# A fused attention and gated feed-forward kernel: direct loads and turns, packed score slabs, new order of the stages

## The chip, the cores and the metric

One core of one Trainium2 chip. The metric is device time in microseconds (us); the kernel before takes 592.26 us (median of three runs, 591.85 to 592.28).

## The reference

Eight batches, eight heads, 576 queries of 64 numbers. Sixteen beacon keys and values stand ahead of the 576 own ones, and a query sees all beacons and the own keys up to its own place. The eight heads' outputs side by side make one token of 512 numbers; 4608 such tokens then go through a gated feed-forward layer of width 1536.

```python
scores = scale * np.matmul(q, k_all.transpose(0, 1, 3, 2))      # k_all = beacon_k, then k
scores = np.where(causal, -1000000000.0, scores)
a = np.exp(scores - scores.max(-1, keepdims=True))
a /= a.sum(-1, keepdims=True) + 1e-09
x = np.matmul(a, v_all).transpose(0, 2, 1, 3).reshape(B * S, H * D)
out = (np.maximum(x @ w_gate, 0.0) * (x @ w_val)) @ w_out
```

## The kernel before, in words

Work goes by pairs of heads: 8 batches of 4 pairs. The loads are all issued by GpSimd (L207, L225), which turns fp32 into bf16 on the way: 24 to 28 transfers a batch, in runs of one head row (64 numbers). Batch 0 is issued first, then the weights (wg and wv in quarters, wo whole), and a whole batch ahead of each batch's first step. The io tiles have two buffers, so batch b+1 is issued when batch b begins.

For each pair TensorE turns q and k (L236, L244; five transposes each) into qT and kT. Four steps follow, each with a score matmul for both heads (L254, `qk`; key rows by query columns, so the scores come out transposed), an exponential on ScalarE (L261), a mask by affine_select on GpSimd (L264), and one step later the product with v (L283, `av`). There the values are the weights of the matmul and the exponentials move through; a second matmul with 64 columns of ones makes the sums of the exponentials on 64 partitions. VectorE then takes the reciprocal of these sums (L290), multiplies (L292) into xT, which is already in the layout that the feed-forward layer wants, and SyncE writes one row of reciprocals to rsum (L294).

The feed-forward layer has nine tiles of 512 tokens (`ffn_tile`). A tile is twelve "ups" (four matmuls with wg at L308, Relu on ScalarE at L311, four matmuls with wv at L314, a product on VectorE at L316) and four "downs" (twelve matmuls at L323, a copy at L326, a store from SyncE at L327). From batch 1 on, one of the sixteen pieces of the preceding tile is put after each attention step: each engine runs its instructions in the order of this program, and a wait of one holds up what stands behind it. Two tiles are left for the end, and before the last but one a count is made of sums that are within range (`count_in_range`); if any is not, a slow general path runs after everything else.

Of the kernel before, what the change touches and what calls it, by code (L numbers as in the profile page):

```python
# [21 lines left out]

STEPS = (
# [5 lines left out]
)  # L29
STEP_COLS = (416, 512, 416, 320)  # L30

CHUNKS = ((0, 256, 0, 0), (256, 256, 1, 2), (512, 64, 3, 3))
CHUNK_OF_STEP = (0, 1, 1, 2)
# [109 lines left out]

@with_exitstack
def kernel(
# [23 lines left out]
    TAIL = Stot - 4 * P  # L169
    M_TILE = 512  # L170
    scale = 1.0 / (D ** 0.5)
    assert (Nb, S, D) == (16, 576, 64)
# [3 lines left out]
    make_identity(nc, ident)  # L176
    ones = const.tile([P, D], BF16, name="ones")
    nc.vector.memset(ones, 1.0)
# [4 lines left out]

    rsum = const.tile([2 * B * NP, S], FP32, name="rsum")

    main = ctx.enter_context(ExitStack())
    io = main.enter_context(tc.tile_pool(name="io", bufs=2))
    tsb = main.enter_context(tc.tile_pool(name="tsb", bufs=2))
    psb = main.enter_context(tc.tile_pool(name="psb", bufs=3))
    nrm = main.enter_context(tc.tile_pool(name="nrm", bufs=3))  # L190
# [3 lines left out]
    aux_ps = main.enter_context(tc.tile_pool(name="aux_ps", bufs=2, space=bass.MemoryType.PSUM))  # L194
    f_ps = main.enter_context(tc.tile_pool(name="f_ps", bufs=2, space=bass.MemoryType.PSUM))


    def load_qkv(b, h0, h1, tiles):
        q_sb, k_sb, v_sb = tiles
        c0, c1 = h0 * D, h1 * D  # L200

        def four(dst, t0, t1, src):
            for t in range(t0, t1):
                part(dst, 0, P, t, src[:, (t - t0) * P:(t - t0 + 1) * P])

        def part(dst, p0, p1, t, src):
            nc.gpsimd.dma_start(  # L207
                dst[p0:p1, t, c0:c1].rearrange("p (h d) -> p h d", d=D),
                src.rearrange("h p d -> p h d"))

        first = P - Nb
        for dst, src, beacon in ((k_sb, k, beacon_k), (v_sb, v, beacon_v)):
            part(dst, 0, Nb, 0, beacon[b, h0:h1])
            part(dst, Nb, P, 0, src[b, h0:h1, 0:first])
            four(dst, 1, 4, src[b, h0:h1, first:first + 3 * P])
            part(dst, 0, TAIL, 4, src[b, h0:h1, first + 3 * P:S])
            if dst is k_sb:
                four(q_sb, 0, 4, q[b, h0:h1, 0:4 * P])
                part(q_sb, 0, S - 4 * P, 4, q[b, h0:h1, 4 * P:S])

    def io_tiles():
        return tuple(io.tile([P, NKT, d_model], BF16, name=n) for n in ("q_sb", "k_sb", "v_sb"))

    def load_w(dst, src, n0, n1):
        nc.gpsimd.dma_start(dst[:, :, n0:n1],  # L225
                            src.rearrange("(ko ki) n -> ki ko n", ki=P)[:, :, n0:n1])


    class Pair:
        pass  # L230

    def prep_q(pr):
        tp = aux_ps.tile([P, 1024], BF16, name="aux")
        for t in range(NKT):
            n = P if t < 4 else S - 4 * P
            nc.tensor.transpose(tp[:, t * P:t * P + n], pr.q[:n, t, pr.c], ident[:n, :n])  # L236
        pr.qT = tsb.tile([P, S], BF16, name="qT")
        nc.vector.tensor_copy(pr.qT, tp[:, :S])

    def prep_k(pr):  # L240
        tp = aux_ps.tile([P, 1024], BF16, name="aux")
        for t in range(NKT):
            n = P if t < 4 else TAIL
            nc.tensor.transpose(tp[:, t * P:t * P + n], pr.k[:n, t, pr.c], ident[:n, :n])  # L244
        pr.kT = tsb.tile([P, NKT * P], BF16, name="kT")
        nc.vector.tensor_copy(pr.kT[:, :Stot], tp[:, :Stot])  # L246
        nc.gpsimd.memset(pr.kT[:, Stot:], 0.0)

    def qk(pr, i):
        s = s_ps.tile([P, 2, 512], FP32, name="s")  # L250
        for (kt, q0, n, c, _, _) in STEPS[i]:
            for a in range(2):
                rows = slice(a * D, (a + 1) * D)
                nc.tensor.matmul(s[:, a, c:c + n], pr.kT[rows, kt * P:(kt + 1) * P],  # L254
                                 pr.qT[rows, q0:q0 + n], start=True, stop=True)
        pr.s[i] = s

    def softmax(pr, i):
        n = STEP_COLS[i]
        p = psb.tile([P, 2, 512], BF16, name="p")  # L260
        nc.scalar.activation(p[:, :, :n], pr.s[i][:, :, :n], AF.Exp, scale=scale)  # L261
        for (kt, q0, _, c, m, base) in STEPS[i]:
            if m:
                nc.gpsimd.affine_select(  # L264
                    out=p[:, :, c:c + m], in_=p[:, :, c:c + m],
                    pattern=[[0, 2], [1, m]], compare_op=ALU.is_ge, fill=0.0,
                    base=base, channel_multiplier=-1)
        pr.p[i] = p

    def av(pr, i):  # L270
        ci = CHUNK_OF_STEP[i]
        cq0, cn, first, last = CHUNKS[ci]
        if i == first:
            pr.o[ci] = aux_ps.tile([P, 2, 256], FP32, name="aux")
        o = pr.o[ci]
        p = pr.p[i]
        for j, (kt, q0, n, c, _, _) in enumerate(STEPS[i]):
            kr = P if kt < 4 else TAIL
            for half in range(2):
                for a in range(2):  # L280
                    rows = slice(a * D, (a + 1) * D)
                    w = pr.v[:kr, kt, pr.c0 + a * D:pr.c0 + (a + 1) * D] if half == 0 else ones[:kr, :]
                    nc.tensor.matmul(  # L283
                        o[rows, half, q0 - cq0:q0 - cq0 + n], w, p[:kr, a, c:c + n],
                        start=(i == first and j == 0 and half == 0),
                        stop=(i == last and j == len(STEPS[i]) - 1),
                        skip_group_check=True)
        if i == last:
            r = nrm.tile([P, 256], FP32, name="r")
            nc.vector.reciprocal(r[:, :cn], o[:, 1, :cn])  # L290
            t0 = pr.b * S + cq0
            nc.vector.tensor_mul(xT[:, pr.p_idx, t0:t0 + cn], o[:, 0, :cn], r[:, :cn])  # L292
            g = 2 * (pr.b * NP + pr.p_idx)
            nc.sync.dma_start(rsum[g:g + 2, cq0:cq0 + cn],  # L294
                              r.rearrange("(a x) n -> a x n", a=2)[:, 0, :cn])


    def ffn_tile(m):
        m0 = m * M_TILE
        st = {}  # L300

        def up(nf):
            def go():
                if nf == 0:
                    st["h"] = fsb.tile([P, NF, M_TILE], BF16, name="hT")
                g = f_ps.tile([P, M_TILE], FP32, name="f")
                for ki in range(KM):
                    nc.tensor.matmul(g, wg[:, ki, nf * P:(nf + 1) * P], xT[:, ki, m0:m0 + M_TILE],  # L308
                                     start=(ki == 0), stop=(ki == KM - 1))
                gs = fsb.tile([P, M_TILE], FP32, name="g")  # L310
                nc.scalar.activation(gs, g, AF.Relu)  # L311
                u = f_ps.tile([P, M_TILE], FP32, name="f")
                for ki in range(KM):
                    nc.tensor.matmul(u, wv[:, ki, nf * P:(nf + 1) * P], xT[:, ki, m0:m0 + M_TILE],  # L314
                                     start=(ki == 0), stop=(ki == KM - 1))
                nc.vector.tensor_mul(st["h"][:, nf, :], gs, u)  # L316
            return go

        def down(ms):
            def go():  # L320
                o = f_ps.tile([P, d_model], FP32, name="f")
                for nf in range(NF):
                    nc.tensor.matmul(o, st["h"][:, nf, ms * P:(ms + 1) * P], wo[:, nf, :],  # L323
                                     start=(nf == 0), stop=(nf == NF - 1))
                ob = osb_p.tile([P, d_model], FP32, name="ob")
                nc.scalar.copy(ob, o)  # L326
                nc.sync.dma_start(out[m0 + ms * P:m0 + (ms + 1) * P, :], ob)  # L327
            return go

        return [up(nf) for nf in range(NF)] + [down(ms) for ms in range(M_TILE // P)]  # L330

    n_m = n_tokens // M_TILE

    def count_in_range():

# [14 lines left out]
    with tc.manual_schedule():  # L350
# [17 lines left out]
        def bind(pr):  # L368
            pr.q, pr.k, pr.v = tiles[pr.b]
# [69 lines left out]
```

## Time and profile before

| | |
|---|---|
| median of three runs | 592.26 us |
| span of the profiled execution | 589.1 us |
| around the span (median less span; no other time of that execution is listed) | 3.2 us |
| TensorE matmul busy | 447.3 us (76%) |
| VectorE / ScalarE / GpSimd busy | 259.4 / 194.9 / 218.1 us |
| mean granted TensorE clock | 0.945 |

The profile is one execution on the chip. Busy times of TensorE hold the latency of each matmul, so the time from one group's start to the next says more than the mean of one. The chain of waits goes back from the last instruction, at each step to what released it.

### The profile page before, as it was taken

The numbers are of one execution on the slowest core, as the hardware profiler recorded it, in microseconds if no ns is written. First come the engines' busy times: TensorE is split into PE (matmuls) and PEld (weight loads), VectorE is DVE, ScalarE is ACT, GpSimd is POOL, SyncE is SP. The second block draws the span as 40 slices with busy tenths as digits, with TensorE's granted clock in tenths as the row PEclk, the third lists the DMA queues.
The fourth block names the chain that finished last, engine by engine and source line by source line (L and its number), as shares of the span: only waits on it lengthen the run. The fifth ranks groups of instructions, "written<-read, shape, count | busy, mean of one in ns | idle before, by whom it ended". The sixth has DMA issues, their size and how long they took to land.

```text
span 589.1 us, 10169 instructions
## 1 busy us (share of the span) xinstructions
PE 447.3 (76%) x4113; PEld 227.8 (39%) x4113; DVE 259.4 (44%) x369; ACT 194.9 (33%) x273; POOL 218.1 (37%) x458
## 2 busy tenths in 40 slices
PE   2000037859995999599969986997799999979995
PEld 1000025525542554355435543553355555424442
DVE  0000027536733673376437543754476576432130
ACT  2000014324432543254425442543244454322321
POOL 9998262471246125621652174217411112000000
PEclk9999999779997999799979996999699999979998
DMA  4669990190059006900890099009901100100102
GB/s 31 40 41 138 202 115 2 14 112 2 3 94 102 1 3 102 94 1 20 96 82 2 21 108 69 2 22 120 57 2 38 39 1 10 65 0 19 53 2 75
DMA packets 127029, 29.45 MB, mean 50 GB/s; under 512 B 116608, under 2 KB 122368, under 8 KB 126976
## 3 DMA queue, kind: packets, MB, share of 16 engines
q0 software_dynamic: 121408, 19.15, 44.4%
q1 hardware_dynamic: 5568, 9.59, 4.4%
q8 instruction: 34, 0.56, 0.4%
q14 instruction: 19, 0.16, 0.1%
HBM read 38.27 MB, written 9.44 MB: 81 GB/s over the span
## 4 chain that ended last, share of the span: by engine, by line
PE 66%; POOL 23%; DMA 6%; DVE 2%; issue 1%; ACT 1%; ACTq 0%; POOLq 0%; DVEq 0%
PE f L308 16%; PE f L314 15%; PE f L323 14%; PE aux L283 11%; POOL v_sb L207 8%; POOL k_sb L207 7%; PE s L254 6%; POOL q_sb L207 5%; DMA wo<-in_moe_w_out_dram 4%; PE aux L236 2%; DMA k_sb<-in_k_dram 2%; PE aux L244 2%; DVE r L290 1%; POOL p L264 1%; ACT p L261 1%
## 5 line engine op out<-in xcount | busy, mean ns | idle before, releaser
L290 DVE RECIPROCAL r<-aux 128x256 f32<-128x256 f32 (+1 forms) x96 | 129.8, 1352 | 160.8 <-PE aux L283 160.7
L261 ACT ACTIVATE p<-s 128x832 bf16<-128x832 f32 (+2 forms) x128 | 110.4, 863 | 245.3 <-PE s L254 245.3
L264 POOL TENSOR_SCALAR_AFFINE_SELECT p<-p 128x224 bf16<-128x224 bf16 (+3 forms) x224 | 67.7, 334 | 273.2 <-ACT p L261 273.2
L283 PE MATMUL aux<-p,v_sb 128*64 128x64 bf16 (+5 forms) x832 | 72.9, 240 | 116.3 <-POOL p L264 111.0
L308 PE MATMUL f<-xT,wg 128*128 128x512 bf16 x432 | 119.5, 400 | 5.0 <-DVE xT L292 4.3
L316 DVE TENSOR_TENSOR hT<-g,f 128x512 bf16<-128x512 f32 x108 | 74.0, 685 | 107.5 <-PE f L314 105.6
L314 PE MATMUL f<-xT,wv 128*128 128x512 bf16 x432 | 114.5, 389 | 0.9 <-DVE hT L316 0.9
L283 PEld LDWEIGHTS <-v_sb 128*64 128x64 bf16 (+1 forms) x832 | 45.6, 116 | 167.6 <-issue 160.1
L323 PE MATMUL f<-wo,hT 128*128 128x512 bf16 x432 | 98.4, 380 | 0.0
L311 ACT ACTIVATE g<-f 128x512 f32<-128x512 f32 x108 | 64.4, 596 | 70.1 <-PE f L308 68.7
L314 PEld LDWEIGHTS <-wv 128*128 128x128 bf16 x432 | 43.4, 100 | 64.4 <-issue 19.3
L283 PE MATMUL aux<-p,ones 128*64 128x64 bf16 (+5 forms) x832 | 64.9, 234 | 0.0
L323 PEld LDWEIGHTS <-hT 128*128 128x128 bf16 x432 | 40.1, 98 | 46.7 <-issue 1.5
L308 PEld LDWEIGHTS <-wg 128*128 128x128 bf16 x432 | 36.9, 100 | 41.6 <-issue 10.6
L254 PE MATMUL s<-qT,kT 64*128 64x64 bf16 (+3 forms) x832 | 49.2, 233 | 0.6 <-DVE kT L246 0.6
L207 POOL DMA_DIRECT2D q_sb<-in_q_dram x55 | 44.2, 890 | 8.0 <-DMA wo<-in_moe_w_out_dram 6.8
L207 POOL DMA_DIRECT2D k_sb<-in_k_dram x55 | 43.8, 858 | 5.7 <-DMA wg<-in_moe_w_gate_dram 3.5
L283 PEld LDWEIGHTS <-ones 128*64 128x64 bf16 (+1 forms) x832 | 45.2, 118 | 0.2
L326 ACT COPY ob<-f 128x512 f32<-128x512 f32 x36 | 21.1, 585 | 72.3 <-PE f L323 72.3
L207 POOL DMA_DIRECT2D v_sb<-in_v_dram x55 | 44.3, 907 | 1.7 <-DMA k_sb<-in_k_dram 1.5
L292 DVE TENSOR_TENSOR xT<-aux,r 128x256 bf16<-128x256 f32 (+1 forms) x96 | 34.3, 358 | 3.3
L254 PEld LDWEIGHTS <-kT 64*128 64x128 bf16 x832 | 25.1, 99 | 12.0 <-issue 7.1
(26 smaller groups left out, 119.4 us busy)
## 6 DMA issues: line engine op xcount, KB each, us to landing
out_dram<-ob SPq DMA_DIRECT2D x36, 256.0 KB
q_sb<-in_q_dram POOLq DMA_DIRECT2D x28, 128.0 KB, 5.7
k_sb<-in_k_dram POOLq DMA_DIRECT2D x21, 128.0 KB, 5.1
v_sb<-in_v_dram POOLq DMA_DIRECT2D x21, 128.0 KB, 4.7
wg<-in_moe_w_gate_dram POOLq DMA_DIRECT2D x4, 384.0 KB, 8.9
wv<-in_moe_w_val_dram POOLq DMA_DIRECT2D x4, 384.0 KB, 10.1
wo<-in_moe_w_out_dram POOLq DMA_DIRECT2D x1, 1536.0 KB, 20.7
rsum<-r SPq DMA_DIRECT2D x64, 2.0 KB
```

The lines of the kernel that those rows point to most:

```text
L207: nc.gpsimd.dma_start(dst[p0:p1, t, c0:c1].rearrange("p (h d) -> p h d", d=D), src.rearrange("h p d -> p h d"))
L254: nc.tensor.matmul(s[:, a, c:c + n], pr.kT[rows, kt * P:(kt + 1) * P], pr.qT[rows, q0:q0 + n], start=True, stop=True)
L261: nc.scalar.activation(p[:, :, :n], pr.s[i][:, :, :n], AF.Exp, scale=scale)
L264: nc.gpsimd.affine_select(out=p[:, :, c:c + m], in_=p[:, :, c:c + m], pattern=[[0, 2], [1, m]], compare_op=ALU.is_ge, fill=0.0, base=base, ...
L283: nc.tensor.matmul(o[rows, half, q0 - cq0:q0 - cq0 + n], w, p[:kr, a, c:c + n], start=(i == first and j == 0 and half == 0), stop=(i == la ...
L290: nc.vector.reciprocal(r[:, :cn], o[:, 1, :cn])
L292: nc.vector.tensor_mul(xT[:, pr.p_idx, t0:t0 + cn], o[:, 0, :cn], r[:, :cn])
L308: nc.tensor.matmul(g, wg[:, ki, nf * P:(nf + 1) * P], xT[:, ki, m0:m0 + M_TILE], start=(ki == 0), stop=(ki == KM - 1))
L311: nc.scalar.activation(gs, g, AF.Relu)
L314: nc.tensor.matmul(u, wv[:, ki, nf * P:(nf + 1) * P], xT[:, ki, m0:m0 + M_TILE], start=(ki == 0), stop=(ki == KM - 1))
L316: nc.vector.tensor_mul(st["h"][:, nf, :], gs, u)
L323: nc.tensor.matmul(o, st["h"][:, nf, ms * P:(ms + 1) * P], wo[:, nf, :], start=(nf == 0), stop=(nf == NF - 1))
```

## The change

Nearly every stage is written anew; the feed-forward arithmetic and the general path stay.

Loads. For batches 0 and 1, k and q come with 9 (or 6 and 3) successive rows in one run, and are turned on TensorE in 64 by 64 pieces (`direct`, `pair_turn`). For batches 2 to 7 the fp32 rows come by SyncE's queue into a stage of six buffers, GpSimd casts them to bf16 (`cast`), and a transposing DMA from SyncE's queue turns them into kq (`turn`). v is staged and cast too. Weights still come by GpSimd's queue, in four parts of columns and wo in three.

Attention. A unit is one pair and one of two groups of queries, 0 to 367 or 368 to 575. Score columns stand in slabs; from batch 2 three slabs are made at once, and one slab may hold parts of two units. The mask is a product with a 0/1 tile on VectorE (`tri`). In `av` the exponentials are now the weights and v with a column of ones is what moves (65 columns), so the sums come out one per query, on its own partition; the reciprocal is of 4 to 6 numbers per partition. The result has tokens on partitions and is turned into xT, by a transposing DMA, or on TensorE for batch 0 and the first group of batch 2.

Order. Feed-forward tiles have 368 and 208 tokens, so that each is ready with its group of queries; downs go by 128 tokens as before. A planner puts ups and downs between attention steps, so that enough is left up to when the next tile is ready; exponentials, masks and `av` stand between pieces of it. PSUM tiles come from a ring of four banks beside two tiles of two banks for scores. The last output tile is made in 384 and 128 columns and stored from ScalarE's queue; all others are stored from GpSimd's queue, the last eight pieces' from SyncE's.

```diff
+SLABS = (
+    ((((2, 240, 128, 0), (0, 0, 368, 128)), 496, 240),
+     (((1, 112, 256, 0),), 256, 128)),
+    ((((4, 496, 80, 0), (0, 368, 208, 80), (1, 368, 208, 288)), 496, 80),
+     (((3, 368, 208, 0), (2, 368, 208, 208)), 416, 128)),
+)
+QROWS = ((0, 112), (112, 128), (240, 128), (368, 128), (496, 80))
+QGROUPS = ((0, 1, 2), (3, 4))
...
+    class Load:
...
+        def issue(self, mark=None):
...
+                    dma(heads[:s1 - s0, 0], rows_of(k, b, s0, s1))
+                    dma(heads[:s1 - s0, 1], rows_of(q, b, s0, s1))
...
+        def cast(self, *engs):
...
+                n = KT4 if self.key[1] == NKT - 1 else P
+                cp(self.c[:n], self.st[:n])
...
+        def turn(self, *cps):
...
+                for i in range(2):
+                    nc.sync.dma_start_transpose(kqs[b % 2][:, i, :, t * P:t * P + n], c[:n, i])
...
+    def direct(c, b, p0, p1, part):
+        r0, r1, _ = PARTS[part]
+        for i, src in enumerate((k, q)):
+            G.dma_start(c[i * D:(i + 1) * D, 2 * p0:2 * p1, r0 * D:r1 * D], runs(src, b, p0, p1, part))
+
+    def pair_turn(c, b, p, part, cps):
...
+        for r in range(r0, r1):
+            for i in range(2):
...
+                for a in range(2):
+                    T.transpose(tps[i][a * D:(a + 1) * D, r - r0], c[rows, 2 * p + a, r * D:(r + 1) * D],
+                                ident[rows, rows])
...
+    class Slab:
...
+        def qk(self, s):
+            self.s = s
+            for u, (kt, q0, n, c) in self.segs:
+                kq = kqs[u.b % 2]
+                for a in range(2):
+                    rows = slice(a * D, (a + 1) * D)
+                    o = s[a] if isinstance(s, list) else s[:, a]
+                    T.matmul(o[:, c:c + n], kq[rows, 0, u.pi, kt * P:(kt + 1) * P],
+                             kq[rows, 1, u.pi, Nb + q0:Nb + q0 + n], start=True, stop=True)
+
+        def exp(self):
+            flat, p = weights(self.cols)
+            self.p = p
+            if isinstance(self.s, list):
+                for a in range(2):
+                    A.activation(p[:, a], self.s[a][:, :self.cols], AF.Exp, scale=scale)
+            else:
+                A.activation(p, self.s[:, :, :self.cols], AF.Exp, scale=scale)
...
+    def mask(u, pool=False, which=(0, 1)):
...
+            V.tensor_mul(p[:, :, :m], p[:, :, :m], tri[:, :, :m])
+
+    def av(u):
...
+                    T.matmul(o[:m, j, a, 0:D + 1], p[:kr, c:c + m],
+                             vs[u.b % 2][:kr, kt, 2 * u.pi + a, 0:D + 1],
+                             start=first, stop=(kt == kts[-1]), skip_group_check=True)
...
+            V.reciprocal(r, o[:m, j0:j1, :, D])
+            V.tensor_mul(
+                u.x[:m, i0:i0 + j1 - j0, u.pi * P:(u.pi + 1) * P].rearrange("p j (a d) -> p j a d", a=2),
+                o[:m, j0:j1, :, 0:D], r.unsqueeze(3).to_broadcast([m, j1 - j0, 2, D]))
+
+    def x_turn(u):
+        for qi in QGROUPS[u.g]:
+            r0, rn = QROWS[qi]
+            nc.sync.dma_start_transpose(xT[:, :, u.b * S + r0:u.b * S + r0 + rn], u.x[:rn, qi, :])
+
+    def x_turn_pair(u, cp):
...
+        for qi in qt:
+            r0, rn = QROWS[qi]
+            T.transpose(tp[:, r0 - c0:r0 - c0 + rn], u.x[:rn, qi, u.pi * P:(u.pi + 1) * P], ident[:rn, :rn])
+        cp(xT[:, u.pi, u.b * S + c0:u.b * S + c1], tp[:, :c1 - c0])
...
+    def ffn_down(i, ms):
...
+        def last(mid=None):
+            for n0, n in ((0, 384), (384, 128)):
+                o = f_ps.tile([P, n], FP32, name="f")
...
+                A.copy(ob, o)
+                A.dma_start(out[rows, n0:n0 + n], ob)
...
+        first.issue()
+        bk[0].issue()
...
+        for p in range(1, NP):
+            direct(c0, 0, p, p + 1, 0)
...
+        scores(g0[0])
+        mask(g0[0], True)
+        chunk(0, 256)
...
+        mask(g0[3], True)
+        chunk(256, 512)
...
+        chunk(512, 1024)
+        vl[0][2].cast(G)
+        chunk(1024, 1536)
...
+        steps = bursts[8:16] + [None] * GAP + bursts[16:8 + NT]
+        steps += [slabs[i:i + 3] for i in range(0, len(slabs), 3)] + [None]
...
+        ready = {}
+        for m0, mn in tiles:
...
+                    ready[e] = pos[last[u] + 1] + (LAG if isinstance(steps[last[u] + 1], list) else 2)
...
+            def fits():
+                return ffn and ready[ffn[0][2]] <= pos[s] and spent + ffn[0][0] / 2 <= want
+
+            def aver():
+                if units:
+                    u = units.pop(0)
+                    av(u)
+                    if (u.b, u.g) == (2, 0):
+                        unturned.append((u, len(ffn)))
+                    elif u.last:
+                        x_turn(u)
```

## Rows read from the trace of the kernel before

**Rows 1.** The profile's chain that ended last, share by engine.
```profile
PE 66%; POOL 23%; DMA 6%; DVE 2%; issue 1%; ACT 1%; ACTq 0%; POOLq 0%; DVEq 0%
```

**Rows 2.** Stretches: length, PE, PEld, DVE, ACT, POOL busy, granted clock, DMA share, GB/s.
```profile
20.00:40.00 20.00, 0.00 (x0) 0.00 (x0) 0.00 (x0) 0.00 (x0) 20.00 (x32) 1.00 0.63 40
...
53.00:63.00 10.00, 0.00 (x0) 0.00 (x0) 0.00 (x0) 0.00 (x0) 5.30 (x8) 1.00 1.31 203
...
180.00:190.00 10.00, 3.93 (x29) 2.33 (x29) 2.59 (x4) 1.04 (x2) 6.30 (x12) 0.66 1.58 101
...
200.00:210.00 10.00, 10.00 (x100) 4.87 (x101) 7.16 (x11) 5.41 (x8) 2.18 (x8) 1.00 0.01 2
```

**Rows 3.** Timeline: start, length, instruction, and the idle time before it.
```profile
8.37 0.29 PE L236 MATMUL aux<-ident,q_sb 128*128 128x128 bf16 x1 [8.37 <-DMA q_sb<-in_q_dram]
...
82.24 0.42 PE L283 MATMUL aux<-p,v_sb 128*64 128x256 bf16 x2 [68.84 <-POOL p L264]
```

**Rows 4.** The chain in order of time, where a batch begins: start, length, what.
```profile
170.91 3.04 POOL k_sb L207 x4
173.94 7.20 DMA k_sb<-in_k_dram
...
181.43 4.19 POOL v_sb L207 x5
```

**Rows 5.** The chain inside a batch, and its last piece.
```profile
198.78 0.51 PE aux L283 x12
199.28 0.29 PE s L254 x6
199.57 0.46 PE aux L236 x5
200.03 0.97 PE f L308 x4
201.00 0.86 PE f L314 x4
201.87 0.56 PE aux L283 x8
202.42 0.25 PE s L254 x10
202.68 0.37 PE aux L244 x5
...
207.40 0.43 PE aux L283 x20
207.83 0.33 PE s L254 x4
...
572.47 10.37 PE f L323 x48
```

**Rows 6.** Groups of instructions by line and shape: busy us, mean ns; idle before.
```profile
L290 DVE RECIPROCAL r<-aux 128x256 f32<-128x256 f32 x64 | 112.2, 1753 | 153.4 <-PE aux L283 153.4
...
L316 DVE TENSOR_TENSOR hT<-g,f 128x512 bf16<-128x512 f32 x108 | 74.0, 685 | 107.5 <-PE f L314 105.6 <-PE aux L283 1.9
L311 ACT ACTIVATE g<-f 128x512 f32<-128x512 f32 x108 | 64.4, 596 | 70.1 <-PE f L308 68.7
L261 ACT ACTIVATE p<-s 128x832 bf16<-128x832 f32 x64 | 55.2, 863 | 180.3 <-PE s L254 180.3
...
L323 PEld LDWEIGHTS <-hT 128*128 128x128 bf16 x432 | 40.1, 98 | 46.7 <-issue 1.5
...
L261 ACT ACTIVATE p<-s 128x1024 bf16<-128x1024 f32 x32 | 32.7, 1023 | 26.4 <-PE s L254 26.4
...
L264 POOL TENSOR_SCALAR_AFFINE_SELECT p<-p 128x256 bf16<-128x256 bf16 x64 | 26.5, 414 | 0.0
```

**Rows 7.** The page's issues: KB each, median us from issue to landing.
```profile
q_sb<-in_q_dram POOLq DMA_DIRECT2D x28, 128.0 KB, 5.7
```

**Rows 8.** Timeline of SyncE's queue: start, length, instruction.
```profile
278.21 0.49 SPq L294 DMA_DIRECT2D rsum<-r  x1
```

More of the change, by code (lines that the diff above doesn't have):

```diff
@@ L193 @@
     s_ps = main.enter_context(tc.tile_pool(name="s_ps", bufs=2, space=bass.MemoryType.PSUM))
[L194 to L229, printed above, removed]
-        pass
[L232 to L279, printed above, removed]
+    class Ring:
+        def __init__(self, name, n, **kw):
+            self.pools = [main.enter_context(tc.tile_pool(name=f"{name}{i}", bufs=1, **kw)) for i in range(n)]
+            self.i = 0
+        def tile(self, shape, dtype, name):
+            self.i += 1
+            return self.pools[self.i % len(self.pools)].tile(shape, dtype, name=name)
@@ new lines, with runs @@
+    PARTS = ((0, 6, 0), (6, R, 384), (0, R, 0))
+    def runs(src, b, p0, p1, part):
+        r0, r1, s0 = PARTS[part]
+        rows = src[b, 2 * p0:2 * p1, s0:s0 + (r1 - r0) * D]
+        return rows.rearrange("h (p r) d -> p h (r d)", r=r1 - r0)
+    def direct(c, b, p0, p1, part):
+        r0, r1, _ = PARTS[part]
+        for i, src in enumerate((k, q)):
+            G.dma_start(c[i * D:(i + 1) * D, 2 * p0:2 * p1, r0 * D:r1 * D], runs(src, b, p0, p1, part))
+    def pair_turn(c, b, p, part, cps):
+        r0, r1, s0 = PARTS[part]
+        n = r1 - r0
+        tps = [f_ps.tile([P, n, D], BF16, name="f") for _ in range(2)]
+        for r in range(r0, r1):
+            for i in range(2):
+                rows = slice(i * D, (i + 1) * D)
+                if isinstance(c, Load):
+                    flat = c.c.rearrange("p a n -> p (a n)")
+                    T.transpose(tps[i][:, r - r0], flat[rows, r * P:(r + 1) * P], ident[rows, rows])
+                    continue
+                for a in range(2):
+                    T.transpose(tps[i][a * D:(a + 1) * D, r - r0], c[rows, 2 * p + a, r * D:(r + 1) * D],
+                                ident[rows, rows])
+        for i in range(2):
+            cps[i](kqs[b % 2][:, i, p, Nb + s0:Nb + s0 + n * D].rearrange("q (p r) -> q p r", r=n),
+                   tps[i].rearrange("q r p -> q p r"))
@@ L280, in av, with qk @@
+    class Burst:
+        pass
+    def qk(u):
+        u.s, u.p, u.parts = [], [], []
+        kq = kqs[u.b % 2]
+        for segs, cols, _ in SLABS[u.g]:
+            s = s_ps.tile([P, 2, 512], FP32, name="s")
+            for (kt, q0, n, c) in segs:
                 for a in range(2):
                     rows = slice(a * D, (a + 1) * D)
[L282 to L302, printed above, removed]
-            def go():
[L304 to L330, printed above, removed]
@@ new lines, in qk, with weights, __init__, mask @@
+                    T.matmul(s[:, a, c:c + n], kq[rows, 0, u.pi, kt * P:(kt + 1) * P],
+                             kq[rows, 1, u.pi, Nb + q0:Nb + q0 + n], start=True, stop=True)
+            u.s.append(s)
+    def weights(w):
+        flat = psb.tile([P, 1024], BF16, name="p")[:, :2 * w]
+        return flat, flat.rearrange("p (a n) -> p a n", a=2)
+    class Slab:
+        def __init__(self, segs, cols, spans):
+            self.segs, self.cols, self.spans = segs, cols, spans
+        def qk(self, s):
+            self.s = s
+            for u, (kt, q0, n, c) in self.segs:
+                kq = kqs[u.b % 2]
+                for a in range(2):
+                    rows = slice(a * D, (a + 1) * D)
+                    o = s[a] if isinstance(s, list) else s[:, a]
+                    T.matmul(o[:, c:c + n], kq[rows, 0, u.pi, kt * P:(kt + 1) * P],
+                             kq[rows, 1, u.pi, Nb + q0:Nb + q0 + n], start=True, stop=True)
+        def exp(self):
[4 more added lines that the diff above has]
+                    A.activation(p[:, a], self.s[a][:, :self.cols], AF.Exp, scale=scale)
+            else:
+                A.activation(p, self.s[:, :, :self.cols], AF.Exp, scale=scale)
+            for u, seg in self.segs:
+                u.parts.append((flat, self.cols, (seg,)))
+        def mask(self):
+            n, m = self.spans
+            if n == 1:
+                V.tensor_mul(self.p[:, :, :m], self.p[:, :, :m], tri[:, :, :m])
+                return
+            d = self.p.rearrange("p a (s c) -> p (a s) c", s=n)[:, :, :m]
+            V.tensor_mul(d, d, tri[:, 0:1, :m].to_broadcast([P, 2 * n, m]))
@@ new lines, in softmax @@
+    def softmax(u, which=(0, 1)):
+        for i in which:
+            cols = SLABS[u.g][i][1]
+            flat, p = weights(cols)
+            A.activation(p, u.s[i][:, :, :cols], AF.Exp, scale=scale)
+            u.p.append(p)
+            u.parts.append((flat, cols, SLABS[u.g][i][0]))
+    def mask(u, pool=False, which=(0, 1)):
+        for i in which:
+            p, m = u.p[i], SLABS[u.g][i][2]
+            if pool:
+                for c, w, base in (((0, P, 0), (P, m - P, Nb)) if m > P else ((0, m, 0),)):
+                    G.affine_select(out=p[:, :, c:c + w], in_=p[:, :, c:c + w], pattern=[[0, 2], [1, w]],
+                                    compare_op=ALU.is_ge, fill=0.0, base=base, channel_multiplier=-1)
+                continue
+            V.tensor_mul(p[:, :, :m], p[:, :, :m], tri[:, :, :m])
@@ new lines, in av @@
+    def av(u):
+        qt = QGROUPS[u.g]
+        o = f_ps.tile([P, len(qt), 2, D + 2], FP32, name="f")
+        blocks = {}
+        for p, w, segs in u.parts:
+            for (kt, q0, n, c) in segs:
+                for j, qi in enumerate(qt):
+                    r0, rn = QROWS[qi]
+                    if q0 <= r0 and r0 + rn <= q0 + n:
+                        blocks[j, kt] = (p, w, c + r0 - q0)
+        first = True
+        for j, qi in enumerate(qt):
+            kts = sorted(kt for (jj, kt) in blocks if jj == j)
+            for a in range(2):
+                for kt in kts:
+                    p, w, c = blocks[j, kt]
+                    c += a * w
+                    m = QROWS[qi][1] if c + P > 2 * w else P
+                    kr = P if kt < 4 else KT4
+                    T.matmul(o[:m, j, a, 0:D + 1], p[:kr, c:c + m],
+                             vs[u.b % 2][:kr, kt, 2 * u.pi + a, 0:D + 1],
+                             start=first, stop=(kt == kts[-1]), skip_group_check=True)
+                    first = False
+        parts = ((0, 3, P),) if u.g == 0 else ((0, 1, P), (1, 2, 80))
+        for j0, j1, m in parts:
+            i0 = qt[j0]
+            r = rall[:m, u.b, u.pi, i0:i0 + j1 - j0]
+            V.reciprocal(r, o[:m, j0:j1, :, D])
+            V.tensor_mul(
+                u.x[:m, i0:i0 + j1 - j0, u.pi * P:(u.pi + 1) * P].rearrange("p j (a d) -> p j a d", a=2),
+                o[:m, j0:j1, :, 0:D], r.unsqueeze(3).to_broadcast([m, j1 - j0, 2, D]))
@@ new lines, with ffn_up, go @@
+    hbs = {}
+    def ffn_up(m0, mn, nf):
+        def go(mid=None):
+            g = f_ps.tile([P, 512], FP32, name="f")
+            for ki in range(KM):
+                T.matmul(g[:, :mn], wg[:, ki, nf * P:(nf + 1) * P], xT[:, ki, m0:m0 + mn],
+                         start=(ki == 0), stop=(ki == KM - 1))
+            gs = fsb.tile([P, 512], FP32, name="g")
+            A.activation(gs[:, :mn], g[:, :mn], AF.Relu)
+            if mid:
+                mid()
+            u = f_ps.tile([P, 512], FP32, name="f")
+            for ki in range(KM):
+                T.matmul(u[:, :mn], wv[:, ki, nf * P:(nf + 1) * P], xT[:, ki, m0:m0 + mn],
+                         start=(ki == 0), stop=(ki == KM - 1))
+            c = m0
+            while c < m0 + mn:
+                i = c // HB
+                e = min((i + 1) * HB, m0 + mn)
+                if i not in hbs:
+                    hbs[i] = fsb.tile([P, NF, HB], BF16, name="hT")
+                V.tensor_mul(hbs[i][:, nf, c - i * HB:e - i * HB], gs[:, c - m0:e - m0], u[:, c - m0:e - m0])
+                c = e
+        return go
@@ new lines, in ffn_down, with go @@
+    def ffn_down(i, ms):
+        rows = slice(i * HB + ms * P, i * HB + (ms + 1) * P)
+        def last(mid=None):
+            for n0, n in ((0, 384), (384, 128)):
+                o = f_ps.tile([P, n], FP32, name="f")
+                for nf in range(NF):
+                    T.matmul(o, hbs[i][:, nf, ms * P:(ms + 1) * P], wo[:, nf, n0:n0 + n],
+                             start=(nf == 0), stop=(nf == NF - 1))
+                ob = osb_p.tile([P, n], FP32, name="ob")
+                A.copy(ob, o)
+                A.dma_start(out[rows, n0:n0 + n], ob)
+        if (i + 1) * HB == n_tokens and ms == HB // P - 1:
+            return last
+        def go(mid=None):
+            o = f_ps.tile([P, d_model], FP32, name="f")
+            for nf in range(NF):
+                T.matmul(o, hbs[i][:, nf, ms * P:(ms + 1) * P], wo[:, nf, :],
+                         start=(nf == 0), stop=(nf == NF - 1))
+            if mid:
+                mid()
+            ob = osb_p.tile([P, d_model], FP32, name="ob")
+            A.copy(ob, o)
+            oq = nc.sync if len(ffn) < 8 else OQ
+            oq.dma_start(out[rows], ob)
+        return go
@@ L406 @@
     main.close()
-    with tc.If(in_range < 2 * B * NP):
+    with tc.If(in_range < P):
         general_path(tc, q, k, v, beacon_k, beacon_v, out, ident, wg, wv, wo)
```

446 lines of the change are left out of this document (362 added, 84 removed), and 5 rows, old and new, of the table STEPS.

## The prediction

> **What bounds the kernel now.** I read the shares of the chain of waits first. The reader is to see that the chain is TensorE for 66% of the span, about 389 us, and that GpSimd (23%) and DMA (6%) hold another 29%, about 171 us [rows 1]. So it is bound twice: by TensorE's work, and by stretches in which TensorE waits for loads. The stretches show where these are. From 20 to 40 us TensorE does nothing at all while GpSimd is busy for the whole 20 us, and from 180 to 190 us it is busy for 3.93 of 10 us; from 200 to 210 us it is full [rows 2]. The timeline says why: the first transpose comes at 8.37 us, and the product with v at 82.24 us has waited 68.84 us for a mask that GpSimd runs only after it has issued all of batch 0, the weights and batch 1 [rows 3]. At the start of a later batch the chain leaves TensorE for GpSimd's issues and a landing, from 170.91 us up to the end of the v issues at 185.62 us [rows 4]. Last I read the chain inside a batch, because it prices TensorE's work as starts of groups and not as latencies [rows 5].
>
> **TensorE's work after, at the granted clock of 1.00** (the 2.4 GHz level).
>
> Feed-forward. Four matmuls of 512 columns take 0.86 us, which is 0.42 ns a column, and the last 48 take 10.37 us, 0.216 us each [rows 5]. Ups: 96 matmuls over 4608 tokens are 442,368 columns, whatever the tile width, 185.8 us. Downs: 432 x 0.216 = 93.3 us. Sum 279 us, as before: the change saves nothing here. A narrower tile could lose it again only if a weight load outlasted its matmul; the smallest, 208 columns, is 87 ns, against 50 ns for the full weight load with its 128 columns that is derived below.
>
> Scores. The groups of 0.33, 0.25 and 0.29 us hold 512, 320 and 416 columns for each of two heads [rows 5]. At 0.42 ns a column that leaves 0.115 us in each, so both heads run at once and a group costs a fixed 0.115 us. After: 1664 columns a pair as before, in two groups: 0.70 + 0.23 = 0.93 us, times 32 pairs is 30 us, against (0.29 + 0.25 + 0.29 + 0.33) x 32 = 37 us.
>
> Product with v. Before: 0.51 + 0.56 + 0.51 + 0.43 = 2.01 us a pair, 64 us [rows 5]; with two passes over 1664 columns it is at the column rate, plus 0.13 to 0.16 us a group. After: a pair has 12 blocks for its first group of queries and 18 for its second, 30 matmuls of 65 columns, 960 in all, each with a weight load of its own 128 columns. That form stands in no row. From below: 65 columns are 27 ns, 26 us. From above: five turns in 0.37 us, 74 ns each with their group's cost in it, 71 us [rows 5]. With the fixed cost taken off, those turns are 50 ns at up to 128 columns, so the weight load is hidden behind them; and twenty matmuls of 64 columns took 0.43 us, about 14 ns each for loads of half the width. I take 33 ns, nearer to the second row because the column count is the same: 32 us, plus 64 groups x 0.15 = 10, together 42 us.
>
> The trace's 50 ns has a rule against it. The Trainium skill, page "TensorE: Matmul & The Clock Gate", section "Back-to-back issue gap", puts a stream of weight loads with matmuls of 128 columns at about 81 ns each; by that the product with v would be 960 x 0.081 = 78 us plus the groups, and my sum 46 us higher. It is weighed as the second rival.
>
> Turns. Before 0.46 + 0.37 us a pair, 27 us [rows 5]. After: for batch 0, 12 + 72 + 48 small turns, for batch 1 144, 276 at 27 ns (64 columns; at most 74) = 7.5 us (to 20); 32 turns of x for batch 0 and the third batch's first group at 54 ns = 2; the beacons and group costs 2. I take 11 us.
>
> Returns from attention to an up cost 0.97 instead of 0.86 us [rows 5]; some 60 of them are 7 us. Sum of TensorE: 279 + 30 + 42 + 11 + 7 = 369 us.
>
> **Around it.** Start: the first k and q come in one transfer each instead of behind twelve, so instead of 8.37 us [rows 3] I take 5 (3 to 8.4). Then cast, turn, copy and scores of the first unit, 2.6 us; four units paced by ScalarE, whose row gives 0.833 ns an element and 0.17 us each (863 and 1023 ns for 832 and 1024 elements [rows 6]), so 1.0 + 0.6 us a unit, with copies 2 us, 8 us; products, reciprocals and turns into xT, 3 us. The first up starts at 19 us (15 to 27), with some 7 us of the counted work done: 12 us idle (8 to 20). The low clock after an idle stretch, 0.66 averaged over 180 to 190 us with the 1.2 GHz level in it [rows 2], falls mostly into that idle time.
>
> Weights: GpSimd issues them behind two masks, yet nothing else moves then; 203 GB/s as written [rows 2] brings wg and wv (3.15 MB) in 15.5 us and wo in 8 more, one twelfth per 1.3 us, while an up of 368 tokens takes 1.24 us. I take 4 us of waiting (0 to 15). GpSimd's 14 us at each batch boundary goes, and the descriptors that it wrote go to SyncE's queue. What is late next, if anything, is that queue, the first rival.
>
> Other engines must hide in about 45 us a batch. ScalarE: 13,312 exponentials in 19 instructions 14.3 us, 24 Relus (596 ns at 512 [rows 6], so 477 and 343 ns) 9.8, copies 2.6: 27 us. VectorE: the reciprocals of 1753 ns [rows 6] vanish, now 4 to 6 numbers wide; products of ups from 685 ns at 512 [rows 6] 13, masks 6, normalizing 5: 24 us; if masks on VectorE ran late, the exponentials' product would wait, at 0.4 us a slab. GpSimd: eight casts of 1024 elements a batch, bounded by 1.6 ns an element (414 ns for 256 [rows 6]) at 13 us, and 4.5 stores. Each is covered. With four banks in a ring instead of two, I take 5 us of short waits (0 to 18).
>
> Tail: the last matmul ends at 582.84 us [rows 5], 6.3 us before the span's end; the last copy is a quarter as wide, so 0.3 us less, 6 us. The 384 and 128 columns are the same matmul time.
>
> Sum: 369 + 12 + 4 + 5 + 6 = 396 us of span, against 589.1; with the 3.2 us between span and median, 399. Against before: TensorE's chain loses 20 us, the start some 65 us, batch boundaries some 90 us.
>
> **Rivals.**
> SyncE's queue is late. Per batch it now runs 18 loads, 10 turns of k and q and 5 of x, in order. A turn waits there for GpSimd's cast, and behind it stand the next loads and the turns of x for which the next feed-forward tile waits. For it: such a wait cost about 14 us a batch before [rows 4]. Against: loads are issued nine steps ahead. With 6 us in each of six batches, 36 more: 435 us (415 to 470).
>
> Weight loads bind in the product with v. For it: a full load is 98 ns by itself [rows 6], and 65 columns cover 27. Against: the five turns at 50 ns. Serial, 960 x (98 - 33) ns = 62 us more: 461 us. The Trainium skill's rule of 81 ns above gives 445.
>
> The transposing DMAs bind, the case on the other side. No row has one; a turn of 128 x 512 bf16 is 128 KB. From below it takes the 0.49 us of an issue [rows 8]. From above it holds the queue to its landing, 5.7 us for 128 KB [rows 7]: 15 x 5.7 + 18 x 0.49 = 94 us a batch instead of 45, six times, 294 more: 693 us. It costs from (45 - 9) / 15 = 2.4 us a turn, and makes the kernel slower than before from 4.6. I take the low end, because plain issues of this queue don't wait for landings. The Trainium skill, "DMA: Bandwidth & Descriptors", section "Latency and other measured facts", measures transposing DMAs at 261 GB/s, by which a turn is an estimated 0.5 us; no run here shows it.
>
> Less than forecast: v's matmuls at 27 ns, no waits for weights or inside, start at 15 us: 399 - 6 - 4 - 5 - 4 = 380, and below 376 only if returns cost nothing too.
>
> **How the numbers follow.** Forecast 0.72, its own range 380 to 416; SyncE's queue late 0.13; weight loads 0.06; transposing DMAs 0.03; below 376 0.06. The time is the forecast's, 399 us. The range 376 to 432 leaves out the upper half of the first rival, the other two and part of the low end, about 0.2. A change under 0.2% can't be told from none here; every case but the DMAs' is far from it: faster 0.96, same 0.01, slower 0.03.
>
> **What would show it.** Right: TensorE above 85% of the chain; the first up near 19 us; pairs of groups of v at some 0.55 and 0.75 us; ups of 368 and 208 columns near 1.24 and 0.70 us; full stretches across batch boundaries at clock 1.00; no GpSimd or DMA piece above 3 us in the chain after 45 us. Wrong: TensorE waiting for kq or xT on a transposing DMA, loads spaced by casts, v's matmuls 50 ns or more apart, or the first up after 27 us.

## The result, and the profile after

The changed kernel takes 375.94 us (373.97 to 376.85, four runs) against 592.06 us: a ratio of 0.6346, 95% interval 0.6326 to 0.6366. Forecast were 399 us, with a range from 376; the time is 23 us less, and just below the range. The profiled execution took 373.97 us with a span of 372.1 us.

The page of the changed kernel: busy time, the slices of TensorE, its granted clock and GpSimd, and the chain by engine and by line, beside [rows 1].

```profile
PE 356.5 (96%) x3769; PEld 238.5 (64%) x3769; DVE 193.0 (52%) x634; ACT 204.5 (55%) x388; POOL 89.8 (24%) x126
...
PE   3789999999999999999999999999999999999995
...
POOL 6862033322233222311412223120321011001100
PEclk9999999999999999999999999999999999999999
...
PE 91%; DMA 5%; POOL 1%; ACT 1%; DVE 1%; issue 0%; SPq 0%; ACTq 0%; POOLq 0%; DVEq 0%
PE f L462 25%; PE f L454 25%; PE f L493 24%; PE f L421 9%; PE s L362 3%; PE f L362 2%; DMA stg<-in_v_dram 2%; DMA wv<-in_moe_w_val_dram 2%; PE s L339 1%; DMA stg<-in_q_dram 1%; PE f L481 1%; PE f L322 0%; DVE hT L470 0%; ACT p L388 0%; POOL cs L308 0%
```

The reader is to see that TensorE is full from the fourth slice to the one before the last, at the 2.4 GHz level throughout, and that GpSimd, 23% of the chain before, is 1%. The lines of the code: L454 and L462 are the two halves of an up, L493 a down, L421 the product with v, L362 and L339 the scores, L322 the small turns. TensorE's stretches, with the same columns as [rows 2], and the first up in the timeline:

```profile
0.00:17.80 17.80, 9.65 (x173) 7.12 (x174) 9.26 (x28) 10.78 (x18) 13.16 (x29) 1.00 1.05 155
20.00:25.00 5.00, 3.93 (x69) 2.12 (x67) 3.02 (x9) 2.64 (x5) 4.24 (x7) 1.00 1.35 199
...
58.00:245.00 187.00, 186.45 (x1924) 125.06 (x1923) 103.88 (x346) 111.20 (x210) 49.46 (x59) 1.00 0.92 169
```
```profile
17.80 1.03 PE L454 MATMUL f<-xT,wg 128*128 128x368 bf16 x4
```

The first up stands at 17.80 us (114.6 us in the kernel before), and from 58 to 245 us, over at least four batch boundaries, TensorE is idle for 0.55 us. The chain inside a batch, beside [rows 5]: start, length, what.

```profile
80.89 0.43 PE s L362 x8
81.32 0.73 PE f L454 x4
...
151.11 0.57 PE f L421 x18
151.68 2.59 PE f L493 x12
154.27 0.62 PE f L454 x4
154.89 0.62 PE f L462 x4
...
156.76 0.28 PE f L362 x4
157.05 0.42 PE s L362 x8
157.47 0.67 PE f L421 x18
158.15 0.69 PE f L454 x4
...
166.44 0.67 PE f L421 x18
167.11 0.63 PE f L454 x4
...
178.47 0.36 PE f L421 x12
...
186.62 0.36 PE f L421 x12
186.98 0.36 PE f L454 x4
187.34 0.36 PE f L462 x4
```

Here is the error of the prediction. A group of the product with v (L421) takes 0.57 us for 18 matmuls and 0.36 for 12, so 31 ns each with nothing fixed, where it follows the feed-forward layer; 0.10 us more where it follows scores (0.67). An up behind it costs no more than its columns (0.62 to 0.63 and 0.36 us for four of 368 and 208); of the 41 such ups in the trace, three took 0.03 to 0.09 us more (0.69 above). An up right behind scores takes 0.73. So a fixed cost goes with the scores, and the stage behind them pays a part of it.

### The profile page after: what moved, and what is told of

The parts are those of the page before. It is cut to its first block, busy times and chain, and to the rows that moved or that the text cites. A ratio compares the mean times of both kernels' runs of the same rounds, so it can differ in the third digit from the quotient of the medians.

```text
span 372.1 us, 9622 instructions
## 1 busy us (share of the span) xinstructions
PE 356.5 (96%) x3769; PEld 238.5 (64%) x3769; DVE 193.0 (52%) x634; ACT 204.5 (55%) x388; POOL 89.8 (24%) x126
## 4 chain that ended last, share of the span: by engine, by line
PE 91%; DMA 5%; POOL 1%; ACT 1%; DVE 1%; issue 0%; SPq 0%; ACTq 0%; POOLq 0%; DVEq 0%
PE f L462 25%; PE f L454 25%; PE f L493 24%; PE f L421 9%; PE s L362 3%; PE f L362 2%; DMA stg<-in_v_dram 2%; DMA wv<-in_moe_w_val_dram 2%; PE s L339 1%; DMA stg<-in_q_dram 1%; PE f L481 1%; PE f L322 0%; DVE hT L470 0%; ACT p L388 0%; POOL cs L308 0%
## 5 line engine op out<-in xcount | busy, mean ns | idle before, releaser
L470 DVE TENSOR_TENSOR hT<-g,f 128x208 bf16<-128x208 f32 (+14 forms) x288 | 92.8, 351 | 82.1 <-PE f L462 52.3
L462 PE MATMUL f<-xT,wv 128*128 128x368 bf16 (+1 forms) x768 | 125.6, 286 | 1.1 <-DVE hT L470 0.7
L454 PE MATMUL f<-xT,wg 128*128 128x368 bf16 (+1 forms) x768 | 125.7, 286 | 0.6 <-ACT g L457 0.5
L457 ACT ACTIVATE g<-f 128x368 f32<-128x368 f32 (+1 forms) x192 | 79.0, 414 | 76.2 <-PE f L454 38.7
L493 PE MATMUL f<-wo,hT 128*128 128x512 bf16 x420 | 94.9, 379 | 0.1
L462 PEld LDWEIGHTS <-wv 128*128 128x128 bf16 x768 | 71.1, 98 | 26.5 <-issue 1.3
L454 PEld LDWEIGHTS <-wg 128*128 128x128 bf16 x768 | 69.4, 98 | 21.6 <-issue 1.3
L493 PEld LDWEIGHTS <-hT 128*128 128x128 bf16 x420 | 39.9, 98 | 44.0
L372 ACT ACTIVATE p<-s 128x992 bf16<-128x992 f32 (+2 forms) x56 | 53.8, 964 | 0.0
L282 POOL CAST c<-stg 128x1024 bf16<-128x1024 f32 (+1 forms) x30 | 31.4, 1045 | 83.1 <-DMA stg<-in_q_dram 80.3
L421 PEld LDWEIGHTS <-p 128*128 128x128 bf16 (+2 forms) x960 | 36.1, 101 | 10.3 <-issue 6.6
L421 PE MATMUL f<-vx,p 128*128 128x65 bf16 (+2 forms) x960 | 41.6, 197 | 0.8 <-DVE p L400 0.6
L430 DVE TENSOR_TENSOR x<-f,rall 128x128 bf16<-128x128 f32 (+1 forms) x96 | 36.3, 378 | 3.4
L388 ACT ACTIVATE p<-s 128x992 bf16<-128x992 f32 (+2 forms) x32 | 26.0, 864 | 4.8 <-PE s L339 4.7
L362 PEld LDWEIGHTS <-kq 64*128 64x128 bf16 x384 | 13.8, 94 | 9.7 <-issue 8.5
L362 PE MATMUL s<-kq 64*128 64x208 bf16 (+4 forms) x256 | 16.0, 249 | 0.0
```

The costliest lines, as they stand in the source:

```text
L282: cp(self.c[:n], self.st[:n])
L362: T.matmul(o[:, c:c + n], kq[rows, 0, u.pi, kt * P:(kt + 1) * P], kq[rows, 1, u.pi, Nb + q0:Nb + q0 + n], start=True, stop=True)
L372: A.activation(p, self.s[:, :, :self.cols], AF.Exp, scale=scale)
L421: T.matmul(o[:m, j, a, 0:D + 1], p[:kr, c:c + m], vs[u.b % 2][:kr, kt, 2 * u.pi + a, 0:D + 1], start=first, stop=(kt == kts[-1]), skip_gro ...
L430: V.tensor_mul(u.x[:m, i0:i0 + j1 - j0, u.pi * P:(u.pi + 1) * P].rearrange("p j (a d) -> p j a d", a=2), o[:m, j0:j1, :, 0:D], r.unsqueeze ...
L454: T.matmul(g[:, :mn], wg[:, ki, nf * P:(nf + 1) * P], xT[:, ki, m0:m0 + mn], start=(ki == 0), stop=(ki == KM - 1))
```

## The experiments

Theory F, formed from these lines: the fixed cost of a group stands only where TensorE goes over to another part of the array, 64 rows (scores) or weights of 64 columns (v in the kernel before), and back. The rival G is what the prediction used: every change of group costs 0.115 to 0.15 us. A matmul's form, below, is the rows of the array and the columns of weights that it uses.

**One matmul ahead of each up, in three forms.** One line in `ffn_up`, ahead of the wg matmuls, which then overwrite its result; one of these three in each kernel:

```diff
+            T.matmul(g[:, :64], wg[:, 0, nf * P:(nf + 1) * P], xT[:, 0, m0:m0 + 64],
+                     start=True, stop=True)        # full
+            T.matmul(g[:, :64], wg[0:D, 0, nf * P:(nf + 1) * P], xT[0:D, 0, m0:m0 + 64],
+                     start=True, stop=True)        # rows
+            T.matmul(g[0:D, :64], wg[:, 0, nf * P:nf * P + D], xT[:, 0, m0:m0 + 64],
+                     start=True, stop=True)        # columns
```

> The changed kernel with one more matmul ahead of each of the 192 ups, of the full form (128 rows, 128 columns of weights, 64 columns moving); its result is overwritten. Theory F (a group costs something extra only where TensorE goes over to another part of the array): 192 x 64 columns x 0.42 ns = 5 us more, 381 us. Rival G, as predicted (every change of group costs 0.115 to 0.15 us): 192 x (0.027 + 0.12) = 28 us more, 404 us.

> The same, but the added matmul uses 64 rows of the array, as the scores do. Theory F: two changes of form each, 0.1 to 0.2 us in all with its 0.027: 24 to 40 us more, 400 to 416 us. Rival G: 28 us more, 404 us, the same as for the full form.

> The same, but the added matmul has weights of 64 columns, as the product with v had in the kernel before. Theory F: 24 to 40 us more, 400 to 416 us. Rival G: 28 us more, 404 us, the same as for the full form.

Measured: full 381.37 us (ratio 0.6442, 0.6429 to 0.6455), rows 416.14 (0.7028, 0.7016 to 0.7041), columns 419.09 (0.7076, 0.7064 to 0.7089). Against 375.5 us of the unedited kernel (below) that is 5.9, 40.6 and 43.6 us for 192 matmuls: 0.031, 0.21 and 0.23 us each. The chains of the three, in this order; L453 is the added matmul:

```profile
161.12 0.04 PE f L453
161.16 0.62 PE f L456 x4
```
```profile
170.20 0.13 PE f L453
170.34 0.73 PE f L456 x4
```
```profile
176.01 0.73 PE f L456 x4
176.74 0.62 PE f L464 x4
177.36 0.15 PE f L453
```

In its own form the matmul costs 0.03 to 0.04 us and the next group keeps its 0.62. In the other forms it takes 0.13 to 0.15 us, and the next group 0.73: 0.1 us on the way out and 0.11 on the way back. It went as F says and not as G says: G had 404 us for all three. The cost does not go with every matmul that leaves part of the array unused: each group of 18 of the product with v holds matmuls with 80 rows or with weights of 80 columns, and still takes 31 ns for each.

```profile
L421 PE MATMUL f<-vx,p 80*128 80x65 bf16 x64 | 11.7, 193 | 0.0
L421 PE MATMUL f<-vx,p 128*80 128x65 bf16 x64 | 7.6, 201 | 0.0
```

**The product with v twice.** `for twice in range(2)` around the matmul of `av`, the last with `stop`.

> Each of the 960 matmuls of the product with v runs twice; product and sum of the exponentials both double, so their ratio stays. Theory F: 31 ns each as in groups of 18 in 0.57 us, 30 us more, 406 us. The rival that weight loads bind: 960 x 98 ns = 94 us more, 470 us; by the Trainium skill's 81 ns (TensorE: Matmul & The Clock Gate, Back-to-back issue gap) 78 us more, an estimate, 454 us.

Measured 405.42 us (0.6844, 0.6823 to 0.6864): 29.9 us for 960 matmuls, 31 ns each. Each of the added matmuls has a weight load of its own in the trace. The groups of 18 grew to 36 in 1.12 us where no scores stand ahead, and to 1.23 behind scores; the 0.1 us does not double. Weight loads of 128 columns are hidden behind 65 columns almost wholly (27 ns at 0.42 ns a column). The 81 ns that the Trainium skill ("TensorE: Matmul & The Clock Gate", "Back-to-back issue gap") gives for a weight load with a matmul of 128 columns, by which the estimate was 78 us more, is not the price of these with 65 columns.

**The parts that the change is named for,** each undone, with the unedited kernel beside them.

```diff
-                    if (u.b, u.g) == (2, 0):
-                        unturned.append((u, len(ffn)))
-                    elif u.last:
+                    if u.last:
...
-            for n0, n in ((0, 384), (384, 128)):
+            for n0, n in ((0, 512),):
...
-        GAP, BB, NT = 1, 9, 8
+        GAP, BB, NT = 1, 9, 56
```

> The changed kernel unedited, beside the next three on the same chip: 376 us by every theory.

> The third batch's first x goes through a transposing DMA like the others. If the next tile's ups then wait for it: 2 to 4 us more (landing 3 us, queue 4 us), 378 to 380 us. If the feed-forward work planned ahead covers it, TensorE saves 12 turns of 54 ns: 375.3 us, no difference.

> The last output tile in one part of 512 columns. The last copy is 0.59 us instead of about 0.27 and the last store 256 instead of 64 KB: 0.3 to 0.8 us more, 376.5 us. Rival: the store's landing is a fixed 2 us whatever its size, so 0.3 us more at most.

> Batches 2 to 7 run unit by unit as batch 1 does, not in packed slabs, and the third batch's first x by DMA. Theory F: 48 score stages instead of 28 at 0.1 to 0.2 us of form changes each, 2 to 4 us more than the kernel with x by DMA alone. If the rival holds that ScalarE's waits decide (a unit's two exponentials stand in one piece ahead of the ups' Relus): 10 us or more.

Measured: unedited 375.5 us (0.6348, 0.6327 to 0.6369), x by DMA 376.83 (0.6373, 0.6350 to 0.6396), last tile whole 375.33 (0.6353, 0.6331 to 0.6375), unpacked with x by DMA 378.71 (0.6404, 0.6384 to 0.6424). The intervals of the first three overlap: neither the turn of the third batch's x nor the last tile's parts can be told from no change. Unpacked is 3.2 us above the unedited kernel, 1.9 above the one with x by DMA alone, whose interval it touches. That is the size of F's 20 score stages more, but not firm. The two profiles point the same way: the spans are 376.7 and 373.4 us, and TensorE is busy for 360.2 and 356.9 us of them, so what was added is TensorE's work and not waiting.

**The kernel before with its loads spread.** `load_qkv` hands its transfers over as a list, and after each step's masks one or two are issued; in a second kernel the weights' transfers are on that list too, first.

```diff
-                        load_qkv(pr.b + 1, 0, H, tiles[pr.b + 1])
+                        load_qkv(pr.b + 1, 0, H, tiles[pr.b + 1], later)
...
                 softmax(pr, i)
+                for _ in range(2 if s % 16 < 6 else 1):
+                    if later:
+                        later.pop(0)()
```

> The kernel before with one edit: the transfers of the next batch are issued one or two after each attention step, behind that step's masks, and no longer all at the batch's start. If GpSimd's issues ahead of the masks make the waits: six boundaries of some 14 us and 28 us at the start go, 84 + 28 = 112 us less, 480 us. Rival: each step's mask now waits behind an issue of 0.9 us, and the stall only spreads: 570 us or more.

> The kernel before with transfers spread as in the run with one edit, and the weights' nine transfers also issued one or two after each of the first steps, instead of ahead of them. The first product with v no longer waits until the last weight has landed: at some 48 us in place of 76, 25 to 28 us less than that run, 495 to 498 us. Rival: the first up still waits for batch 1, whose transfers now come later: no gain, 523 us.

Measured 522.85 us (0.8834, 0.8799 to 0.8869) and 513.07 us (0.8662, 0.8614 to 0.8710). The first edit takes 70 us, not 112. Where [rows 4] had a boundary, its chain stays on TensorE (from 160 to 198 us); but in the start it still waits for GpSimd behind the weights, and the first up comes at 99.8 us instead of 114.6. So 15 of the 70 us are in the start, and some 55 lay on the boundaries. With the weights behind the first masks too, the first v comes at 47.79 us as expected, yet the wait returns three steps later:

```profile
54.63 0.87 ACT p L266
56.41 18.97 DMA wo<-in_moe_w_out_dram
75.67 3.33 POOL q_sb L208 x4
```

By the chain GpSimd's next issues come only after wo has landed, and masks stand behind them; 10 us are gained, not 25.

**SyncE's queue, the first rival.** Each turn of k and q issued twice in a row; then, as that made turns wait for their own landing, the preceding piece's k, or k and q, once more.

```diff
+                if t:
+                    for i in range(2):
+                        nc.sync.dma_start_transpose(kqs[b % 2][:, i, :, (t - 1) * P:t * P], Load.prev[:, i])
+                Load.prev = c
```

> The changed kernel with each transposing DMA of k and q issued twice, 60 more on SyncE's queue. They hold the queue 1.26 us each, so a batch's 18 loads and 15 turns are 29 us of some 44, and 10 more turns make 41.6. If the queue has that room: no difference beyond 1 us, 376 us. The first rival of the prediction (the queue is nearly late): waits of 4 us or more in each of six batches, 400 us or more.

> The changed kernel with the turn of k of each piece but a batch's last issued again behind the next piece's turns, when its first landing is past: 24 more transposing DMAs, 4 a batch, which hold SyncE's queue 1.26 us each; a batch's 29 us become 34 of 44. If the queue has that room: 376 us. If the first rival of the prediction was near: 380 us or more.

> The same for k and q: 48 more, 8 a batch, 39 of 44 us. If the queue has that room: up to 378 us. If the queue's own time binds: 8 x 1.26 = 10 us a batch more less what room there is, 400 us or more. Where a turn waits for its own earlier landing, as in the run with each issued twice in a row, the queue is held longer; that is taken away here.

Measured: 60 more turns 446.89 us (0.7551, 0.7521 to 0.7582), 24 more 410.83 (0.6928, 0.6882 to 0.6974), 48 more 434.53 (0.7339, 0.7297 to 0.7381): 71, 35 and 59 us. My expectation of room fell. SyncE's queue in the changed kernel as it stands (start, length, instruction), in a full stretch and in one with gaps, and its turns by tile (min/median/max ns), show why:

```profile
205.86 0.58 SPq L255 DMA_DIRECT2D stg<-in_q_dram  x1
206.57 3.42 SPq L437 DMA_TRANSPOSE xT<-x  x2
210.09 5.12 SPq L296 DMA_TRANSPOSE kq<-c  x4
215.26 0.58 SPq L254 DMA_DIRECT2D stg<-in_k_dram  x1
215.88 0.58 SPq L255 DMA_DIRECT2D stg<-in_q_dram  x1
...
218.35 3.36 SPq L296 DMA_TRANSPOSE kq<-c  x2
...
255.71 1.74 SPq L244 DMA_DIRECT2D stg<-in_v_dram  x2
263.91 2.50 SPq L296 DMA_TRANSPOSE kq<-c  x2
```
```profile
L296 SPq DMA_TRANSPOSE kq<-c x60: 1174/1258/2591, 58.8 to 282.9; - x60
```

The queue has stretches without gaps, and from 58 to 245 us its issues add up to 161 of 187 us. A turn holds it 1.26 us, and 24 more are 30 us of its time, near the 35 us measured. The stretch from 58 to 245 us with 24 more, and waits (who waited for whom, us in total, times, longest): TensorE's for kq in that kernel's whole span, then the queue's own for casts in the changed kernel:

```profile
58.00:245.00 187.00, 165.59 (x1638) 108.61 (x1644) 92.50 (x303) 96.42 (x179) 41.85 (x49) 0.94 0.84 153
```
```profile
PE f L365 <- DMA kq<-c: 17.7, 2, 10.8
PE s L365 <- DMA kq<-c: 9.0, 3, 4.7
```
```profile
SPq L296 <- POOL c L282: 14.5, 5, 6.4
```

TensorE now waits for kq: 165.59 us busy where it was 186.45, and the granted clock is 0.94 where it was 1.00. Queue time turned into time nearly one for one in all three runs: 71, 35 and 59 us for 76, 30 and 60 us of turns. The queue is not simply full: with 24 more turns its issues fill 151 of the same 187 us, so its gaps, in which it waits for casts and, in the turns of x, for VectorE, did not take the new turns up. How much of the added time is the queue's own and how much comes of these waits standing in it in order is not separated: no run has turns on a second queue, or casts or x earlier.

**Weights earlier,** as an attempt at a faster kernel: the second part of wg and wv is issued ahead of the second k and q transfers, and the fourth unit's mask goes to VectorE.

```diff
+        chunk(256, 512)
         direct(c0, 0, 0, NP, 1)
...
-        mask(g0[3], True)
-        chunk(256, 512)
+        mask(g0[3])
```

> The changed kernel with the second part of wg and wv issued ahead of the second k and q transfers and of the fourth unit's mask, which goes to VectorE. The chain runs over this part's landing at 23.54 us. If the start is bound there: 1 to 1.5 us less, 374.5 us. Rival: TensorE only waited 0.36 us for it, so 0.4 us less at most, no difference that shows.

Measured 382.19 us (0.6442, 0.6418 to 0.6466): 6.7 us slower, which the expectation and its rival both left out. The chain at its start:

```profile
16.79 13.35 DMA stg<-in_v_dram
30.19 0.62 POOL vx L267
30.85 0.52 PE f L421 x6
```

The last v rows of batch 0 are now issued behind 512 KB more of weights (as written) and take 13.35 us to land; the product with v waits for their cast up to 30.85 us. In the unedited kernel that cast began at 21.37 us. TensorE's waits for the two casts of v are 1.10 and 3.15 us, and the granted clock, 1.00 in the unedited kernel, is 0.50 (the 1.2 GHz level) from 32 to 36 us, some 2 us more. No version here is measurably faster than the changed kernel.

## Why the prediction was wrong

The mechanism was right: TensorE's work bounds the kernel, boundaries and start lose their waits, and the first up at 17.80 us (19 forecast) and the tail of 5.1 us (6) came as worked out. What failed is the price of TensorE's stages: a fixed cost was put on every change of group, and the runs show it only on changes to and from 64 rows or 64 columns of weights. By step:

- "0.15 us a group" for the product with v, 10 of its 42 us. That fixed cost was read from [rows 5] as a cost of any group. It was the old form's, with weights of 64 columns. The new form is that of the feed-forward layer, and only the 38 of its groups that stand right behind scores pay 0.1 us. The matmul itself, taken at 33 ns, measured 31. By these prices the product with v is 34 us.
- "Some 60 returns are 7 us". An up behind v costs nothing extra; only one right behind scores does (0.73), and there are three of those.
- Scores: 0.115 us in 64 groups, 30 us. The fixed cost was right (0.43 us for 752 columns, 0.32 us at the column rate), but from batch 2 three slabs stand together, and the trace has 43 score stages, not 64: 27 us.
- Turns, 11 us. Small ones at "27 ns (64 columns)": 36 of them take 0.41 us, 11 ns each with the group's fixed cost in it. The code puts them on different quarters of the array, which would let them run beside each other; no run has them on one quarter. By this price, with 0.09 us for two turns of x, the turns are some 5 us.

```profile
29.66 0.09 PE f L445 x2
...
47.95 0.41 PE f L322 x36
48.36 0.43 PE s L339 x6
```

These four are 8 + 7 + 3 + some 6 = 24 us, about the whole of the 23 us by which the time lay below the forecast; all four erred the same way. The rest nearly cancels. In the chain behind 23.58 us, some 7 us before the last matmul lie on other engines, where 9 were counted for weights and inner waits; the tail is 0.9 us shorter; the feed-forward work was some 2 us more, all of it in ups (0.715 us for one of 208 columns, where 0.70 was forecast, and 2.59 us for a down, as forecast). The chance of 0.06 for a time below 376 us named the failing term itself ("returns cost nothing"), and gave it too little.

Point by point of the rest. The price of the weight loads was right, and the second rival fell. The first rival did not happen: TensorE has no wait for kq or xT in the trace. But the argument against it, loads issued nine steps ahead, left the queue's own time out. At the 0.49 us a turn that the third rival's low end took, a batch's 18 loads and 15 turns are 16 us of 45; a turn measured 1.26, and the queue is held 86% of the stretch above. Its landing of 3.0 to 3.3 us stayed off the path, since two turns issued 1.26 us apart are under way at once. The estimate of 0.5 us a turn from the Trainium skill's 261 GB/s ("DMA: Bandwidth & Descriptors", "Latency and other measured facts") was for the transfer; what the queue is held is 1.26 us here. The split of the gain, 20 us of TensorE, 65 of start, 90 of boundaries, was off: spread loads give 70 us, of which 55 at boundaries; the first up moves by 97 us; and from the kernel with loads and weights spread (513 us, first up at 90.8) to the changed one (376, 17.8), 73 us are the earlier first up, and the stretch behind it is 64 us shorter. As these two do not do the same work ahead of the first up, that split is rough. TensorE's part of the chain fell from 389 us (66% of 589.1) to 339 us (91% of 372.1), 50 us and not 20; some 7 of the 369 us forecast were counted in the start.

## What to carry to other kernels

Price a matmul stage by the form of its neighbours: here 0.1 us was paid each time that TensorE passed between the form of the feed-forward layer and one of 64 rows or 64 columns of weights, so a stage in the form of the rest saves it twice, beyond its columns. Read a fixed cost off a row only together with what stands before and after it. And where a rival was dismissed by an issue time, measure the issue of that very instruction: a queue that is held 86% of the time showed nothing in the chain until a little more was put on it.

## What the runs showed of the hardware

- Going to 64 rows or to 64 weight columns for one matmul and back costs 0.18 to 0.20 us beside its 0.03.
- Matmuls of 65 columns with a weight load of 128 columns each run 31 ns apart; a group of 36 turns of 64 by 64, placed on the four quarters of the array, takes 0.41 us, 11 ns each.
- A transposing DMA of 128 x 512 bf16 holds SyncE's queue 1.26 us (a plain load mostly 0.43 to 0.7) and lands in 3.0 to 3.3.
- Rows of 256 bytes issued behind large weight transfers took 13.35 us to land, where v's loads take 3.5 to 5.0 us (medians by size) in the unedited kernel.
